# Merging two row blocks' score products into one burst, and the sinks' value product into one stacked split product, in a fused attention, feed-forward and expert kernel

## The chip, the cores and the metric

One core of one Trainium2 chip runs the kernel. The metric is the device time of one execution in microseconds (us); lower is better. Three executions of the kernel before gave 1141.84, 1143.38 and 1145.58 us, median 1143.38 us.

## The reference, cut to what matters

Three stages follow each other: attention with a window of 128 positions and 4 sinks (4 batches, 8 heads, 768 positions, head size 64), a feed-forward layer with `h * cos(h)`, and a top-1 mixture of 8 experts. Only the first stage is touched:

```python
scores = scale * np.matmul(q, k.transpose(0, 1, 3, 2))
keep = is_sink | in_window
scores = np.where(keep, scores, -1000000000.0)
scores = scores - np.max(scores, axis=-1, keepdims=True)
a = np.exp(scores)
a = a / (np.sum(a, axis=-1, keepdims=True) + 1e-09)
return np.matmul(a, v)
```

`is_sink` holds for the first key positions, `in_window` for the last 128 up to the query's own. Everything is float32.

## The kernel before, in words

The tokens are worked on in eight halves, numbered `hb` from 0 to 7: batch `hb // 2`, and in it the first or the second 384 positions (`half = hb % 2`). A half has three row blocks of 128 queries (`t`) and four pairs of heads (`pr`). One attention pair passes through three stages, all of them generators that `attn_front` (L392) makes:

- the front: q and k are loaded, transposed on TensorE, and copied out of PSUM. From the fourth half on (`hb >= STACK`, STACK is 3) they are split in a rounded part and a rest, both in fp32r (`qT[0]`, `qT[1]`, `kT[0]`, `kT[1]`).
- `mid` (L476): `scores` (L490) is called once for each row block. It takes one PSUM bank per head, issues the products for both heads (three per head where q and k are split), and then one VectorE operation per head (L502) that adds the mask, negates, and takes the row's extremum. A row block has 272 keys (128 before, 16 sinks' places, 128 own). In a first half, block 0 has its own 128 keys alone, and block 1 has 272. Six exponentials on ScalarE follow.
- `rest` (L520): VectorE normalizes (L525 on; for `hb < 3` GpSimd multiplies), TensorE transposes the probabilities (`pt`), and the sinks' part goes a way of its own. A copy `pc` (L575) gathers the sinks' columns of both heads (16 each, 32 together), one transpose per row block goes to `pz` (L578), ScalarE copies it to `sp` (L579), and a product with `vs_n` (values of the sinks, one head's in rows 0 to 15 and columns 0 to 63, the other's in rows 16 to 31 and columns 64 to 127) opens the accumulation in `po` (L592). It is a float32 product for each head, into 64 of the 128 partitions. It covers 384 columns in a second half (three row blocks) and 128 columns in a first half (block 2 only, `t0 = 2`; the sinks of blocks 0 and 1 lie in their windows). The products of values and probabilities (L596) are added to the same bank.

`vs_n2` and `sp2` are two buffers each, taken in turn by pairs (`pr % 2`); zeros are written into them once at the start. The sinks' values are loaded into `vs_n` by a DMA on SP's queue (L433).

What sets the order: from the third half on the sequence is written out as mid of a pair, front of the next pair, rest of the pair. Between the `yield`s of this sequence steps of the feed-forward layer of the half before are woven in (`run_ffn`, L1015 on), in proportion to the weight that each yield gives (`steps(hb)`). A step of the feed-forward layer has 12 products `hp` of 384 columns, VectorE and ScalarE operations on `ch` (L142, L145, L688, L148), a rounded part `g_h` on ScalarE, a rest `g_l` on GpSimd, and two steps later 12 products `y` of 512 columns. Then the framework orders each engine's instructions at compile time, by program order and by a model of when each is ready, and places the waits. All of PSUM's eight banks are shared out; from the second half on the attention and the routing take three of them in turn (`ps_a`, L113).

TensorE's operations pass through the helper `mm` (L135, recorded as L136); VectorE's and GpSimd's through `ts`, `stt` and `tt` (L140 to L148).

Of the kernel before, what the change touches and what calls it, by code (L numbers as in the profile page):

```python
# [11 lines left out]
F32 = DT.float32  # L12
F32R = DT.float32r
# [3 lines left out]
AF = mybir.ActivationFunctionType  # L17
ALU = mybir.AluOpType
AX = mybir.AxisListType

P = 128
# [15 lines left out]
STACK = 3  # L37
# [24 lines left out]
def kernel(  # L62
# [17 lines left out]
    B, H, S, D = q.shape  # L80
# [5 lines left out]
    HALF = S // 2  # L86
    NQ = HALF // P
# [4 lines left out]
    NS = 16  # L92
    SEG = P + NS
    W3 = 2 * P + NS
    SCALE = 1.0 / math.sqrt(D)
# [39 lines left out]
    def mm(o, l, r, start, stop):  # L135
        PE.matmul(o, l, r, start=start, stop=stop)  # L136
# [10 lines left out]
    def tt(e, o, a, b, op):  # L147
        e.tensor_tensor(out=o, in0=a, in1=b, op=op)  # L148
# [92 lines left out]
    sp2 = [apool.tile([P, HALF], F32, name=f"sp{i}") for i in range(2)]  # L241
    for i in range(2):
        DVE.memset(vs_n2[i], 0.0)
        POOL.memset(sp2[i], 0.0)
# [68 lines left out]
    def steps(hb):  # L313
        return STEPS_0 if hb <= 1 else STEPS_1
# [80 lines left out]
    def attn_front(hb, pr):  # L395
# [8 lines left out]
        def folded(t):  # L404
            return whole and (half == 1 or t > 1)

        vs_n, sp = vs_n2[pr % 2], sp2[pr % 2]
        n_ps = [0]

        def psb(name):  # L410
            if hb > 0 or not extra:
                return ps_a(name)
            n_ps[0] += 1
            return ps_y(n_ps[0] % NQ, name)
# [59 lines left out]
        def mid():  # L474
            nonlocal mx, sm, Pb, Pt, cols
            kf = [t.rearrange("p t s -> p (t s)") for t in kT]  # L476
            if extra:
                Pb = [[pb_x[2 * t + j][:, 0:W3] for j in range(2)] for t in range(NQ)]
            else:
                Pt = late_pool().tile([P, NQ, 2, W3], F32, name="Pb2") if hb >= PB2 and pr % 2 else apool.tile([P, NQ, 2, W3], F32, name="Pb", bufs=PBB)  # L480
                Pb = [[Pt[:, t, j] for j in range(2)] for t in range(NQ)]
            mx = apool.tile([P, 2 * NQ], F32, name="mx", bufs=2)
            sm = apool.tile([P, 2 * NQ], F32, name="sm", bufs=2)

            def cols(t):
                if half == 0:
                    return (SEG, W3, 0) if t == 0 else (0, W3, (t - 1) * SEG)
                return 0, W3, t * SEG

            def scores(t, js):  # L490

                c0, c1, o = cols(t)
                w = c1 - c0
                qs = slice(t * P, (t + 1) * P)
                ps = {j: psb("ps") for j in js}
                parts = ((0, 0), (0, 1), (1, 0)) if stack else ((0, 0),)
                for n, (x, y) in enumerate(parts):
                    for j in js:
                        mm(ps[j][:, 0:w], qT[x][hr[j], qs], kf[y][hr[j], o:o + w], n == 0, n == len(parts) - 1)
                for j in js:  # L500
                    i = 2 * t + j
                    DVE.tensor_tensor_reduce(  # L502
                        out=Pb[t][j][:, c0:c1], in0=ps[j][:, 0:w], in1=masks[:, min(half * NQ + t, 2), c0:c1],
                        scale=-SCALE, scalar=3.0e38, op0=ALU.add, op1=ALU.min, accum_out=mx[:, i:i + 1])

            for t in range(NQ):
                if hb >= PAIRED:
                    scores(t, (0, 1))
                    yield 2 * steps(hb)[1]
                else:  # L510
                    for j in range(2):
                        scores(t, (j,))
                        yield steps(hb)[1]
            for t in range(NQ):
                for j in range(2):
                    c0, c1, _ = cols(t)
                    i = 2 * t + j
                    ACT.activation(out=Pb[t][j][:, c0:c1], in_=Pb[t][j][:, c0:c1], func=AF.Exp, scale=-1.0,  # L518
                                   bias=mx[:, i:i + 1], accum_out=sm[:, i:i + 1])
            yield steps(hb)[2]  # L520
        def rest():
# [44 lines left out]
                    POOL.tensor_copy(rb[t].rearrange("p (j d) -> p j d", d=D),  # L566
                                     sm[:, 2 * t:2 * t + 2].unsqueeze(2).to_broadcast([P, 2, D]))
            t0 = 2 if half == 0 else 0
            pc = apool.tile([P, NQ, 2, NS], F32, name="pc")
            if extra:  # L570
                for t in range(t0, NQ):
                    for j in range(2):
                        POOL.tensor_copy(pc[:, t, j], Pb[t][j][:, P:SEG])
            else:
                (POOL if hb < NPOOL else DVE).tensor_copy(pc[:, t0:], Pt[:, t0:, :, P:SEG])  # L575
            pz = psb("pz")
            for t in range(t0, NQ):
# [816 lines left out]
```

## Time and profile before

| what | value |
|---|---|
| median of three executions | 1143.38 us (1141.84 to 1145.58) |
| profiled execution, its own time | 1143.94 us |
| its span, first to last instruction | 1142.2 us |
| granted TensorE clock, mean | 0.996 |
| TensorE (PE) busy | 1103.6 us, 97% |
| VectorE (DVE) busy | 678.3 us, 59% |
| ScalarE (ACT) busy | 602.5 us, 53% |
| GpSimd (POOL) busy | 224.5 us, 20% |
| DMA | mean 99 GB/s |

A busy share is taken over the whole span. The four stretches of the kernel are the first halves' attention with the weight conversion (0 to about 231 us), the halves 3 to 7 with the feed-forward layer woven in (about 231 to 690 us), the feed-forward layer alone with the first expert's weights (690 to 1000 us) and the experts (from 1000 us). In rows of the timeline, the time given for a matmul is its own duration through a pipeline, and the next one starts before it ends: what an instruction costs TensorE is read from the distance of starts. A row with "x4" is four instructions of one kind one behind the other; a float32 product is two instructions.

### The profile page before, as it was taken

Reading aid. Unit: us, or ns where it says so; the run is one execution under the profiler, and the core shown is the slowest. Engines: PE = TensorE matmul, PEld = TensorE weight load, DVE = VectorE, ACT = ScalarE, POOL = GpSimd, SP = SyncE. Lnnn points to the kernel's source line nnn. Section 1 sums busy time; section 2 is a strip of 40 time slices with the busy share of each in tenths; the row PEclk is TensorE's granted clock in tenths of the full one; section 3 lists DMA queues with packets and bytes.
Section 4 is the critical chain, followed back from the end, with each engine's and each line's share of the span. In section 5 each row is a group of like instructions: output and inputs, shape, how many; then the busy total and the mean of one; then the engine's idle time right before and its main releaser. Section 6 shows DMA issues by size and latency. Waiting matters only on the chain.

```text
span 1142.2 us, 20840 instructions
## 1 busy us (share of the span) xinstructions
PE 1103.6 (97%) x6624; PEld 928.0 (81%) x6624; DVE 678.3 (59%) x2126; ACT 602.5 (53%) x1239; POOL 224.5 (20%) x273
## 2 busy tenths in 40 slices
PE   5989999999999999999999999999999999999995
PEld 3667777888888878888888879999889998899984
DVE  6778888666876766776676774746742125522210
ACT  5878887656665566665657553434322225422221
POOL 1232224211111111111111111322121211221110
PEclk9999999999999999999999999999999999999998
DMA  6567665422332322323233223633151115111110
GB/s 150 151 197 196 195 195 158 109 73 68 95 74 76 105 72 64 108 70 75 63 104 79 62 75 102 230 93 89 60 203 40 57 58 184 41 58 39 40 43 23
DMA packets 136083, 113.40 MB, mean 99 GB/s; under 512 B 95727, under 2 KB 103919, under 8 KB 135920
## 3 DMA queue, kind: packets, MB, share of 16 engines
q1 hardware_dynamic: 131600, 97.87, 30.3%
q0 software_dynamic: 4320, 13.65, 3.7%
q8 instruction: 66, 1.08, 0.4%
q14 instruction: 97, 0.79, 0.2%
HBM read 151.06 MB, written 19.67 MB: 149 GB/s over the span
## 4 chain that ended last, share of the span: by engine, by line
PE 85%; DVE 5%; DMA 5%; ACT 2%; issue 1%; POOL 1%; SPq 0%; DVEq 0%; POOLq 0%; ACTq 0%
PE hp L136 23%; PE y L626 22%; PE m_h L136 10%; PE m_y L136 10%; PE ps L136 5%; PE po L136 5%; DMA out_dram<-m_ot,m_ids 3%; DMA cv_in<-in_moe_w_in_dram 1%; PE pl L754 1%; PE pq L444 1%; PE pt L546 1%; PE yT L743 1%; PE pk L454 1%; PE m_a L1093 1%; PE mh L136 1%
## 5 line engine op out<-in xcount | busy, mean ns | idle before, releaser
L148 POOL TENSOR_TENSOR g_l<-ch,g_h 128x384 fp32r<-128x384 f32 x128 | 132.4, 1035 | 558.2 <-ACT g_h L698 435.4
L136 PE MATMUL hp<-xT_h,wi_h 128*128 128x384 f32 x512 | 188.3, 368 | 2.7 <-DVE ch L148 2.7
L136 PE MATMUL hp<-xT_h,wi_l 128*128 128x384 f32 x512 | 174.5, 341 | 0.0
L136 PE MATMUL hp<-xT_l,wi_h 128*128 128x384 f32 x512 | 174.0, 340 | 0.0
L626 PE MATMUL y<-wo,g_h 128*128 128x512 f32 x384 | 158.6, 414 | 0.0
L626 PE MATMUL y<-wo_l,g_h 128*128 128x512 f32 x384 | 155.6, 405 | 0.0
L626 PE MATMUL y<-wo,g_l 128*128 128x512 f32 x384 | 154.1, 401 | 0.2 <-POOL g_l L148 0.2
L688 ACT ACTIVATE ch<-ch,cols 128x384 f32<-128x384 f32 x128 | 78.7, 616 | 116.6 <-DVE ch L145 116.0
L136 PE MATMUL m_y<-wi_h,hT 128*128 128x512 f32 x416 | 132.5, 393 | 0.7 <-ACT m_ot L1135 0.6
L145 DVE SCALAR_TENSOR_TENSOR hT<-m_h,hT 128x256 fp32r<-128x256 f32 x88 | 37.3, 424 | 151.0 <-ACTq L1287 102.4
L136 PEld LDWEIGHTS hp<-xT_h,wi_h 128*128 128x128 f32 x512 | 96.7, 189 | 18.1 <-issue 7.2
L142 DVE TENSOR_SCALAR ch<-hp 128x384 int32<-128x384 f32 x128 | 70.9, 554 | 59.1 <-PE hp L136 46.3
L698 ACT ACTIVATE g_h<-ch 128x384 fp32r<-128x384 f32 x128 | 66.4, 520 | 67.8 <-DVE ch L148 46.0
L136 PEld LDWEIGHTS hp<-xT_l,wi_h 128*128 128x128 f32 x512 | 97.0, 189 | 3.7 <-issue 0.2
L136 PEld LDWEIGHTS hp<-xT_h,wi_l 128*128 128x128 f32 x512 | 96.7, 189 | 1.2 <-issue 0.9
L148 DVE TENSOR_TENSOR ch<-ch,hp 128x384 f32<-128x384 f32 x128 | 70.4, 550 | 39.9 <-ACT ch L688 39.5
L136 PEld LDWEIGHTS m_y<-wi_h,hT 128*128 128x128 f32 x416 | 78.1, 188 | 17.0 <-issue 1.0
L518 ACT ACTIVATE Pb<-Pb,mx 128x272 f32<-128x272 f32 (+1 forms) x168 | 82.9, 494 | 10.9 <-DVE mx L502 10.0
L626 PEld LDWEIGHTS y<-wo,g_l 128*128 128x128 f32 x384 | 72.2, 188 | 14.8 <-POOL g_l L148 0.8
L626 PEld LDWEIGHTS y<-wo,g_h 128*128 128x128 f32 x384 | 72.4, 189 | 13.8 <-issue 3.3
L502 DVE CUSTOM_DVE_ANT_0 Pb<-ps,masks 128x272 f32<-128x272 f32 (+1 forms) x168 | 63.7, 411 | 31.7 <-PE ps L136 31.2
L136 PE MATMUL ps<-kT,qT 64*128 64x272 f32 (+1 forms) x504 | 72.6, 350 | 8.9 <-ACT kT L468 7.0
(276 smaller groups left out, 2236.0 us busy)
## 6 DMA issues: line engine op xcount, KB each, us to landing
rw<-in_moe_w_dram SPq DMA_DIRECT2D x112, 512.0 KB
wo_l<-wl_scr SPq DMA_DIRECT2D x122, 256.0 KB
cv_in<-in_moe_w_in_dram SPq DMA_DIRECT2D x16, 512.0 KB
cv_out<-in_moe_w_out_dram SPq DMA_DIRECT2D x16, 512.0 KB
y_scr<-yt SPq DMA_DIRECT2D x24, 256.5 KB
xT_h<-xg_h SPq DMA_DIRECT2D x32, 192.0 KB
xT_l<-xg_l SPq DMA_DIRECT2D x32, 192.0 KB
qn<-in_q_dram SPq DMA_DIRECT2D x56, 96.0 KB
```

What stands on the lines that cost most here:

```text
L136: PE.matmul(o, l, r, start=start, stop=stop)
L142: e.tensor_scalar(out=o, in0=i, scalar1=s1, scalar2=s2, op0=op0, op1=op1)
L145: e.scalar_tensor_tensor(out=o, in0=i0, scalar=s, in1=i1, op0=op0, op1=op1)
L148: e.tensor_tensor(out=o, in0=a, in1=b, op=op)
L444: PE.transpose(pq[:, t * P:(t + 1) * P], qn[:, t].rearrange("p j d -> p (j d)"), ident)
L454: PE.transpose(pk[:, t * P:(t + 1) * P], kn[:, t].rearrange("p j d -> p (j d)"), ident)
L502: DVE.tensor_tensor_reduce(out=Pb[t][j][:, c0:c1], in0=ps[j][:, 0:w], in1=masks[:, min(half * NQ + t, 2), c0:c1], scale=-SCALE, scalar=3.0 ...
L518: ACT.activation(out=Pb[t][j][:, c0:c1], in_=Pb[t][j][:, c0:c1], func=AF.Exp, scale=-1.0, bias=mx[:, i:i + 1], accum_out=sm[:, i:i + 1])
L546: PE.transpose(pt2[:, j * P:(j + 1) * P], Pb[t][j][:, SEG:W3], ident)
L626: i = PE.matmul(o, l, r, start=start, stop=stop)
L688: ACT.activation(out=ch, in_=ch, func=AF.Sin, scale=TWO_PI, bias=half_pi)
L698: ACT.activation(out=gh, in_=ch, func=AF.Copy)
```

## The change: what it does

From `hb = 3` on (`stacked`, the same bound as `stack`):

1. `scores` takes a list of row blocks. In a first half (`hb` 4 and 6) blocks 0 and 1 are done in one call: 12 products in one burst, block 0's 128 columns and block 1's 272 behind each other in one bank for each head, and then four VectorE operations. Block 2 stays a call of its own. Second halves stay as they were.
2. The sinks' product is one fp32r product for both heads. `pc3` holds the rounded probabilities twice and the rest once (96 columns in place of 32), so that `sp_r` has 96 rows; `vsr2` holds in rows 0 to 31 the rounded values, in 32 to 63 their rest, and in 64 to 95 the rounded values again. VectorE makes `pc3` with a copy and a subtraction, GpSimd makes `vsr` with two copies and a subtraction for every pair. New tiles are zeroed by GpSimd once, when the front of half 3 is first traced; `sp_r` takes the place of `sp` (same tag).

```diff
+        stacked = hb >= STACK
+        if stacked and not vsr2:
+            for i in range(2):
+                vsr2.append(apool.tile([P, 2 * D], F32R, name=f"vs_r{i}"))
+                sp2[i] = apool.tile([P, HALF], F32R, name=f"sp_r{i}", tag=f"sp{i}")
+                POOL.memset(vsr2[i].bitcast(F32), 0.0)
+                POOL.memset(sp2[i].bitcast(F32), 0.0)
...
-            def scores(t, js):
...
+            def scores(tl, js):
+
                 ps = {j: psb("ps") for j in js}
-                parts = ((0, 0), (0, 1), (1, 0)) if stack else ((0, 0),)
-                for n, (x, y) in enumerate(parts):
+                at_ = 0
+                spans = []
+                for t in tl:
+                    c0, c1, o = cols(t)
+                    w = c1 - c0
+                    spans.append((t, c0, c1, at_, w))
+                    qs = slice(t * P, (t + 1) * P)
+                    parts = ((0, 0), (0, 1), (1, 0)) if stack else ((0, 0),)
+                    for n, (x, y) in enumerate(parts):
+                        for j in js:
+                            mm(ps[j][:, at_:at_ + w], qT[x][hr[j], qs], kf[y][hr[j], o:o + w], n == 0, n == len(parts) - 1)
+                    at_ += w
+                for t, c0, c1, at_, w in spans:
                     for j in js:
...
+            groups = ((0, 1), (2,)) if stack and half == 0 else ((0,), (1,), (2,))
+            for tl in groups:
                 if hb >= PAIRED:
-                    scores(t, (0, 1))
-                    yield 2 * steps(hb)[1]
+                    scores(tl, (0, 1))
+                    yield 2 * len(tl) * steps(hb)[1]
...
-            pc = apool.tile([P, NQ, 2, NS], F32, name="pc")
-            if extra:
+            if stacked:
+                pc = apool.tile([P, NQ, 3, 2, NS], F32R, name="pc3")
+                pv = Pt[:, t0:, :, P:SEG]
+                DVE.tensor_copy(pc[:, t0:, 0:2], pv.unsqueeze(2).to_broadcast([P, NQ - t0, 2, 2, NS]))
+                tt(DVE, pc[:, t0:, 2], pv, pc[:, t0:, 0].bitcast(F32), ALU.subtract)
+                vsr = vsr2[pr % 2]
+                i0, i1, i2 = [slice(i * 2 * NS, (i + 1) * 2 * NS) for i in range(3)]
+                POOL.tensor_copy(vsr[i0], vs_n[i0])
+                POOL.tensor_copy(vsr[i2], vs_n[i0])
+                tt(POOL, vsr[i1], vs_n[i0], vsr[i0].bitcast(F32), ALU.subtract)
...
+            nr = (6 if stacked else 2) * NS
             for t in range(t0, NQ):
-                PE.transpose(pz[0:2 * NS, t * P:(t + 1) * P], pc[:, t].rearrange("p j s -> p (j s)"), ident)
-            ACT.activation(out=sp[0:2 * NS, t0 * P:], in_=pz[0:2 * NS, t0 * P:HALF], func=AF.Copy)
+                pi_ = pc[:, t].rearrange("p g j s -> p (g j s)").bitcast(F32) if stacked else pc[:, t].rearrange("p j s -> p (j s)")
+                PE.transpose(pz[0:nr, t * P:(t + 1) * P], pi_, ident)
+            ACT.activation(out=sp[0:nr, t0 * P:], in_=pz[0:nr, t0 * P:HALF], func=AF.Copy)
...
-            for j in range(2):
+            if stacked:
+                mm(po[:, t0 * P:HALF], vsr2[pr % 2], sp[:, t0 * P:HALF], True, False)
+            for j in range(0 if stacked else 2):
                 mm(po[hr[j], t0 * P:HALF], vs_n[:, j * D:(j + 1) * D], sp[:, t0 * P:HALF], True, False)
```

## Rows read from the trace of the kernel before

**Rows 1.** The page: busy time, share of the span and instructions of each engine.

```profile
PE 1103.6 (97%) x6624; PEld 928.0 (81%) x6624; DVE 678.3 (59%) x2126; ACT 602.5 (53%) x1239; POOL 224.5 (20%) x273
```

**Rows 2.** Windows: length, busy of PE, PEld, DVE, ACT, POOL (instructions), clock, DMA, GB/s.

```profile
231.00:326.00 95.00, 94.85 (x583) 78.67 (x582) 66.80 (x230) 60.86 (x118) 16.36 (x16) 1.00 0.30 79
...
690.00:1000.00 310.00, 306.49 (x1824) 275.86 (x1823) 149.67 (x438) 109.89 (x213) 63.92 (x60) 1.00 0.32 104
```

**Rows 3.** Waits of TensorE, 231 to 690 us: total us, times, longest.

```profile
PE pz L578 <- DVE pc L575: 0.6, 2, 0.5
```

**Rows 4.** Tile sp, 200 to 1000 us: ns min/median/max, first and last start, forms.

```profile
L136 PE MATMUL po<-sp,vs_n x80: 272/486/537, 225.8 to 683.4; 128*64 128x384 f32 x48, 128*64 128x128 f32 x32
```

**Rows 5.** TensorE's timeline at a second half's sinks' product: start, us, instruction.

```profile
250.25 0.34 PE L136 MATMUL hp<-xT_l,wi_h 128*128 128x384 f32 x1
250.42 0.34 PE L136 MATMUL hp<-xT_h,wi_l 128*128 128x384 f32 x1
250.69 0.87 PE L136 MATMUL po<-sp,vs_n 128*64 128x384 f32 x4
251.39 1.47 PE L136 MATMUL po<-pT,vn 128*64 128x128 f32 x16
```

**Rows 6.** TensorE's timeline at a first half's sinks' product.

```profile
345.07 0.44 PE L136 MATMUL po<-sp,vs_n 128*64 128x128 f32 x4
345.34 1.25 PE L136 MATMUL po<-pT,vn 128*64 128x256 f32 x12
```

**Rows 7.** TensorE's timeline at the routing's fp32r products of 192 columns.

```profile
307.01 0.48 PE L136 MATMUL pi<-rB,rA 128*128 128x192 f32 x3
307.33 0.36 PE L136 MATMUL hp<-xT_h,wi_h 128*128 128x384 f32 x1
```

**Rows 8.** TensorE's timeline at the score products of blocks 0 and 1, half 4.

```profile
349.43 0.34 PE L136 MATMUL hp<-xT_h,wi_l 128*128 128x384 f32 x1
349.69 0.55 PE L136 MATMUL ps<-kT,qT 64*128 64x128 f32 x6
350.17 0.44 PE L136 MATMUL hp<-xT_h,wi_h 128*128 128x384 f32 x1
350.45 0.34 PE L136 MATMUL hp<-xT_l,wi_h 128*128 128x384 f32 x1
...
351.59 0.65 PE L136 MATMUL ps<-kT,qT 64*128 64x272 f32 x6
352.17 0.50 PE L626 MATMUL y<-wo,g_h 128*128 128x512 f32 x1
```

**Rows 9.** Timeline: sinks' copy in rows 5's pair; copy and transpose in a first half.

```profile
248.45 0.22 DVE L575 COPY pc<-Pb 128x96 f32<-128x96 f32 x1
...
385.55 0.18 DVE L575 COPY pc<-Pb 128x32 f32<-128x32 f32 x1
...
386.68 0.27 PE L578 MATMUL pz<-ident,pc 128*32 128x128 f32 x1
```

**Rows 10.** TensorE's timeline at the sinks' transposes of rows 5's pair.

```profile
249.04 0.49 PE L578 MATMUL pz<-ident,pc 128*32 128x128 f32 x3
249.28 0.48 PE L626 MATMUL y<-wo,g_h 128*128 128x512 f32 x1
249.60 0.40 PE L626 MATMUL y<-wo_l,g_h 128*128 128x512 f32 x1
```

**Rows 11.** Groups by form on VectorE: busy us, mean ns, idle before.

```profile
L148 DVE TENSOR_TENSOR ch<-ch,hp 128x384 f32<-128x384 f32 x128 | 70.4, 550 | 39.9 <-ACT ch L688 39.5
...
L575 DVE COPY pc<-Pb 128x96 f32<-128x96 f32 x12 | 2.5, 212 | 0.0
...
L148 DVE TENSOR_TENSOR hT<-m_t,hT 128x128 fp32r<-128x128 f32 x8 | 2.3, 289 | 2.1 <-ACT hT L1123 2.1
```

**Rows 12.** Groups by form on GpSimd: busy us, mean ns, idle before.

```profile
L148 POOL TENSOR_TENSOR g_l<-ch,g_h 128x384 fp32r<-128x384 f32 x128 | 132.4, 1035 | 558.2 <-ACT g_h L698 435.4 <-PE ps L136 32.6 <-PE yT L743 28.4
```

**Rows 13.** GpSimd's timeline around the product of rows 5.

```profile
251.09 1.00 POOL L148 TENSOR_TENSOR g_l<-ch,g_h 128x384 fp32r<-128x384 f32 x1 [2.49 <-ACT g_h L698]
```

More of the change, by code (lines that the diff above doesn't have):

```diff
@@ L240 @@
     vs_n2 = [apool.tile([P, 2 * D], F32, name=f"vs_n{i}") for i in range(2)]
-    sp2 = [apool.tile([P, HALF], F32, name=f"sp{i}") for i in range(2)]
+    sp2 = [apool.tile([P, HALF], F32, name=f"sp{i}", tag=f"sp{i}") for i in range(2)]
+    vsr2 = []
     for i in range(2):
@@ L488, in cols @@
                 return 0, W3, t * SEG
-            def scores(t, js):
-                c0, c1, o = cols(t)
-                w = c1 - c0
-                qs = slice(t * P, (t + 1) * P)
+            def scores(tl, js):
                 ps = {j: psb("ps") for j in js}
-                parts = ((0, 0), (0, 1), (1, 0)) if stack else ((0, 0),)
-                for n, (x, y) in enumerate(parts):
-                    for j in js:
[L499 to L504, printed above, removed]
@@ L506, in mid @@
-            for t in range(NQ):
+                at_ = 0
[10 more added lines that the diff above has]
+                    at_ += w
@@ new lines, in scores @@
+                for t, c0, c1, at_, w in spans:
+                    for j in js:
+                        i = 2 * t + j
+                        DVE.tensor_tensor_reduce(
+                            out=Pb[t][j][:, c0:c1], in0=ps[j][:, at_:at_ + w], in1=masks[:, min(half * NQ + t, 2), c0:c1],
+                            scale=-SCALE, scalar=3.0e38, op0=ALU.add, op1=ALU.min, accum_out=mx[:, i:i + 1])
+            groups = ((0, 1), (2,)) if stack and half == 0 else ((0,), (1,), (2,))
+            for tl in groups:
@@ L507, in mid @@
                 if hb >= PAIRED:
-                    scores(t, (0, 1))
-                    yield 2 * steps(hb)[1]
+                    scores(tl, (0, 1))
+                    yield 2 * len(tl) * steps(hb)[1]
                 else:
                     for j in range(2):
-                        scores(t, (j,))
-                        yield steps(hb)[1]
+                        scores(tl, (j,))
+                        yield len(tl) * steps(hb)[1]
             for t in range(NQ):
@@ L568, in rest @@
             t0 = 2 if half == 0 else 0
-            pc = apool.tile([P, NQ, 2, NS], F32, name="pc")
-            if extra:
+            if stacked:
[8 more added lines that the diff above has]
+                tt(POOL, vsr[i1], vs_n[i0], vsr[i0].bitcast(F32), ALU.subtract)
+            else:
+                pc = apool.tile([P, NQ, 2, NS], F32, name="pc")
+            if stacked:
+                pass
+            elif extra:
                 for t in range(t0, NQ):
@@ L590, in rest @@
             po = psb("po")
-            for j in range(2):
+            if stacked:
+                mm(po[:, t0 * P:HALF], vsr2[pr % 2], sp[:, t0 * P:HALF], True, False)
+            for j in range(0 if stacked else 2):
                 mm(po[hr[j], t0 * P:HALF], vs_n[:, j * D:(j + 1) * D], sp[:, t0 * P:HALF], True, False)
```

## The prediction

> **What bounds the kernel now.** I read the page first: TensorE is busy for 97% of the span, no other engine for more than 59% [rows 1]. Since that is an average, I read the stage that the change touches next, the halves 3 to 7. In its first 95 us TensorE is busy for 94.85, VectorE for 66.80 and GpSimd for 16.36, at full granted clock [rows 2]. Then I asked what TensorE waits for between 231 and 690 us: the whole answer is two waits, 0.6 us together, both of the sinks' transposes for the copy `pc` [rows 3]. So here the time is the sum of what TensorE issues, and a change is worth what it takes off that sum, less any wait that it makes. What comes behind has no fixed date: TensorE is busy for 306 of the next 310 us [rows 2], and later loads are issued by the flow of the work, so I let a gain reach the end whole.
>
> **How prices are read.** A matmul's own time overlaps the next one's, so I use distances of starts. An fp32r product of 384 columns costs 0.17 us (250.25 to 250.42) [rows 5].
>
> **The sinks' product, second halves.** The four instructions (two heads, two per float32 product) start at 250.69 and the next product at 251.39: 0.70 us [rows 5]. There are 48 such instructions, 12 pairs [rows 4]. In their place comes one fp32r product of 384 columns with a 128 x 128 stationary side, the shape of `hp`: 0.17 us. The step from `hp` to the 64-column form costs something too, 250.42 to 250.69 is 0.27 us, 0.10 over the usual distance [rows 5]. That step doesn't vanish: it moves behind the new product, since the next `po` products keep their form. So 0.53 us a pair are saved, **6.3 us**. Upper bound of the new price: 0.27 us, if it pays that step a second time; then 5.2 us.
>
> The Trainium skill (TensorEngine Tiling (Array Packing), Theoretical Speedup) speaks against this part: where the stationary side has at most 64 columns, array tiles side by side give up to twice the speed, and the change gives that up. By it the new product would cost double, 0.35 us, and the sum below would lose 2.1 us. Rows 5 fit the tiles' side of it (two heads in 0.70 us); but the new product does both heads in one pass through the block structure of the values, so I don't take the doubled price.
>
> **The sinks' product, first halves.** Four instructions of 128 columns take 0.27 us (345.07 to 345.34) [rows 6], 32 of them, 8 pairs [rows 4]. The new one is an fp32r product of 128 columns. The nearest rows are products of 192 columns, three in 0.32 us, 0.11 each [rows 7]; by columns it would be 0.07. I take 0.08: 0.19 saved, **1.5 us** (bounds 1.3 and 1.6).
>
> **The burst.** Around block 0's six products, 349.43 to 349.69 is 0.26 us and 350.17 to 350.45 is 0.28 us where 0.17 is usual: 0.09 to get into the 64-row form and 0.11 to get out of it. The bodies are 0.48 us for block 0 and 0.58 us for block 1 [rows 8]. In all 8 first-half pairs (halves 4 and 6, four each) these two bursts stand apart, as here. One burst saves one entry and one exit, 0.20 us, **1.6 us** over 8 pairs. Lower bound nothing, if the order at compile time parts the burst; I see no reason for more, as each product loads its own stationary side in either order. Block 0's VectorE operations now wait for block 1's products, and four run together; nothing behind them on VectorE made TensorE wait before [rows 3], so I cost this at nothing. Without that cover the `ch` operations, 0.55 us each [rows 11], are late and TensorE waits for `hp`'s banks. Two banks fewer are taken per pair, which can only ease the turn of three.
>
> **The transposes.** Three cost 249.04 to 249.60 less the 0.23 us of one `y`, 0.33 us [rows 10]. They have 96 stationary columns in place of 32; the moving side, the identity's 128 columns, is the same, so I add nothing (bounds: nothing, and 0.04 us on each of 44, 1.8 us, which is a distance of 0.15 in place of 0.11).
>
> **VectorE's longer chain.** `pc` took 0.21 us for 96 elements. Its successor writes 192, and a subtraction of 96 elements follows (64 and 32 in first halves). The nearest subtraction takes 0.29 us for 128 [rows 11], so I estimate 0.25, and 0.08 for the wider copy: 0.33 us more in front of the transposes. In the pair of rows 5 the copy ended at 248.67 and the transposes began at 249.04 [rows 9, 10], so some 0.1 to 0.2 us of this is covered, and 0.2 stands open, in 12 second-half pairs. First halves have more room: the shortest of their eight leads is 386.68 - 385.73 = 0.95 us [rows 9]. Against a wait: the compile-time order moves the transposes behind more `y` or `hp` products if its model sees the longer chain. Bounds: nothing, and 12 x 0.33 = 4.0 us. I take 0.12 a pair, **1.4 us lost**, nearer to nothing because only two such waits are there now [rows 3].
>
> **GpSimd.** Three operations on 32 x 128 per pair: by columns each is a third of `g_l`, which takes 1.04 us for 384 [rows 12], so some 1.1 us together as an estimate, 20 times. GpSimd is idle for five sixths of the stage [rows 2], and the sinks' values were loaded a pair of heads earlier, so they hide, provided that they stand ahead of the right `g_l` (rival 2). The load of `vs_n` for two pairs later, on SP's queue, now waits for GpSimd's readers in place of TensorE's product, which is no later. Four one-time zeroings in front of half 3, at most 1 us each by `g_l`, are hidden by the same idle time; one waits for the third half's last sinks' product, and at worst 1 us shows.
>
> **The sum.** 6.3 + 1.5 + 1.6 - 1.4 = 8.0 us. The profiled execution took 1143.94 us around a span of 1142.2, so it would take 1135.9. The median of the three runs stands 0.56 us below it, so the time to be measured is 1135.4 us. With all bounds at one side the gain is 9.5, at the other 6.5 - 6.8, about nothing. A measurement of this kernel can tell some 0.3%, 3.4 us.
>
> **Rivals.**
>
> 1. *The wait takes the gain.* If the transposes' place isn't moved, 12 pairs lose 0.33 us and the gain is 5.4 us: 1138.0. If one of the `ch` operations (0.55 us) [rows 11] gets in between VectorE's copy and its subtraction, 0.88 us are lost in 12 pairs, 10.6 us against 9.4: 1144.6, no change. For it: VectorE is busy for 70% of the stage, and the copy already ends when the transposes start. Against it: program order puts the two next to each other.
> 2. *Slower: GpSimd's queue.* The new product waits for three GpSimd operations. In the same pair as above, a `g_l` starts at 251.09, 0.40 us behind the product, having waited 2.49 us for ScalarE [rows 13]. If the three stand behind it in the queue, they are done at 252.09 + 1.1 = 253.2, and the product that was due at 250.69 holds TensorE for 2.5 us. That decides as soon as 4 pairs of 20 have it (10 us against 9.4); with 10 pairs the loss is 25 - 8 = 17 us: 1160. Against it: in program order the three stand ahead of that `g_l`, and their data are there long before.
> 3. *The burst is parted*, or pays for its form inside: the gain lacks 1.6 us and the time is 1137.0. The doubled price of the untiled product would give 1137.5.
>
> **How the numbers follow.** Forecast 0.68 (its own range 1132 to 1139), rival 3 0.08, rival 1 with its first size 0.06, with its second 0.11, rival 2 0.07. Faster by over 0.3% are the first three, 0.82; within 0.3% is the second size of rival 1, 0.11; slower is rival 2, 0.07. The range goes from 1131.5 (the largest gain of 9.5, and 2 us of scatter between executions) to 1141, which takes in rival 3, rival 1's first size and a little of the second; what it leaves out is rival 2, most of rival 1's second size and tails.
>
> **What would show it.** In the profile after, one `po<-sp_r` instruction of 384 columns with 0.17 us to the next start and 0.1 more behind it; 12 `ps` instructions in a row with one entry and one exit; TensorE's waits in that stage still below 2 us; the stage from half 3 to 7 shorter by 8 us and the stretches behind it as long as before. The prediction is wrong if TensorE waits for `pc3` by 0.3 us or more in most pairs, if it waits for `vs_r` at all, or if the stage gets shorter and a later stretch longer.

## The result, and the profile after

The changed kernel takes 1136.2 us (median of six executions, 1133.28 to 1137.13) against 1145.81 us for six executions of the kernel before beside it: ratio 0.9915 [0.9901, 0.9929], faster by 9.6 us. A second set gave 1136.52 us and 0.9919 [0.9903, 0.9934]. The profiled execution has a span of 1134.2 us and took 1136.03 us.

**Page and windows.** The page's line on engines, then the windows with the columns of [rows 2]; beside them stand [rows 1, 2].

```profile
PE 1095.3 (97%) x6564; PEld 928.8 (82%) x6564; DVE 678.1 (60%) x2146; ACT 602.1 (53%) x1239; POOL 247.0 (22%) x337
```

```profile
231.00:326.00 95.00, 94.16 (x573) 78.82 (x572) 68.30 (x235) 60.88 (x118) 20.44 (x28) 1.00 0.31 81
690.00:1000.00 310.00, 306.75 (x1852) 277.14 (x1851) 148.46 (x437) 110.06 (x216) 64.38 (x60) 1.00 0.31 102
```

TensorE has 60 instructions fewer (20 pairs, four turned into one) and 8.3 us less to do, and is as full as it was. GpSimd's 64 new instructions cost it 22.5 us.

**TensorE's waits, 225 to 690 us**, answering to [rows 3]:

```profile
PE pz L608 <- DVE pc L148: 1.0, 3, 0.5
PE pz L608 <- ACT pT L573: 0.6, 1, 0.6
PE pt L561 <- DVE kT L148: 0.5, 1, 0.5
PE pt L561 <- DVE pT L148: 0.5, 1, 0.5
```

2.6 us in place of 0.6. That is more than the 2 us that the prediction set as a sign, but little against the work removed.

**The sinks' way in a second half.** TensorE's timeline, the pair of [rows 5, 10]:

```profile
251.15 0.49 PE L608 MATMUL pz<-ident,pc 128*96 128x128 f32 x3
251.40 0.42 PE L136 MATMUL hp<-xT_h,wi_h 128*128 128x384 f32 x1
...
252.01 0.34 PE L136 MATMUL hp<-xT_h,wi_h 128*128 128x384 f32 x1
252.22 0.44 PE L136 MATMUL po<-sp_r,vs_r 128*128 128x384 f32 x1
252.59 1.52 PE L136 MATMUL po<-pT,vn 128*64 128x128 f32 x16
```

The new product has 0.37 us to the next start, where [rows 5] have 0.70. It stands 1.07 us behind its transposes; in the kernel before it was 1.65 (249.04 to 250.69). That is close: in nine of the 12 second-half pairs TensorE's weight load waits for ScalarE's copy, and there the product has 0.37 us; the other three have 0.27. Of the tile view of `sp_r`, the line on what TensorE waited for:

```profile
  ACT sp_r L609: 2.0, 9
```

**VectorE in that pair**, answering to [rows 9], and its groups by form, answering to [rows 11]:

```profile
249.86 0.30 DVE L587 CAST pc<-Pb 128x192 fp32r<-128x192 f32 x1
250.09 0.54 DVE L145 SCALAR_TENSOR_TENSOR ch<-hp,ch 128x384 f32<-128x384 f32 x1
250.54 0.24 DVE L148 TENSOR_TENSOR pc<-Pb,pc 128x96 fp32r<-128x96 f32 x1
```

```profile
L587 DVE CAST pc<-Pb 128x192 fp32r<-128x192 f32 x12 | 3.5, 292 | 0.0
L148 DVE TENSOR_TENSOR pc<-Pb,pc 128x96 fp32r<-128x96 f32 x12 | 2.9, 244 | 0.0
```

A `ch` operation does get in between copy and subtraction, here and in nine more of the 12 second-half pairs. In this pair 12 `hp` and `y` products stand between the last transpose of the probabilities and the sinks' transposes, where the kernel before has nine, so the longer chain costs TensorE little as a wait.

One first-half pair (half 4's first) went otherwise:

```profile
320.05 1.00 POOL L148 TENSOR_TENSOR g_l<-ch,g_h 128x384 fp32r<-128x384 f32 x1 [4.58 <-ACT g_h L730]
320.17 0.93 DVE L148 TENSOR_TENSOR pc<-Pb,pc 128x32 fp32r<-128x32 f32 x1
320.54 0.60 ACT L573 ACTIVATE pT<-pt 128x512 f32<-128x512 f32 x1
321.24 0.29 PE L608 MATMUL pz<-ident,pc 128*96 128x128 f32 x1 [0.57 <-ACT pT L573]
```

Five other VectorE operations stand between its copy and this subtraction. The subtraction takes 0.93 us, where the other seven first-half pairs have 0.18 to 0.20; it starts 0.12 us behind a `g_l` of GpSimd and ends 0.05 us behind it. The changed kernel's repetition and E6 have the same in this pair (0.94 and 0.93 us). TensorE loses 0.8 us ahead of this transpose. The trace names ScalarE's `pT`, but that ends only 0.04 us after the subtraction, so it doesn't tell which of the two held TensorE.

**First half.** The sinks' product answering to [rows 6], then one burst answering to [rows 8]:

```profile
345.23 0.22 PE L136 MATMUL po<-sp_r,vs_r 128*128 128x128 f32 x1
345.38 1.30 PE L136 MATMUL po<-pT,vn 128*64 128x256 f32 x12
```

```profile
305.62 0.39 PE L658 MATMUL y<-wo,g_l 128*128 128x512 f32 x1
305.94 0.98 PE L136 MATMUL ps<-kT,qT 64*128 64x128 f32 x12
306.84 0.44 PE L136 MATMUL hp<-xT_h,wi_h 128*128 128x384 f32 x1
307.12 0.34 PE L136 MATMUL hp<-xT_l,wi_h 128*128 128x384 f32 x1
```

0.15 us in place of 0.27. The merged body takes 0.90 us (305.94 to 306.84); the two apart take 0.48 + 0.58 = 1.06 [rows 8]. It still pays one step in (305.62 to 305.94, 0.32 us where `y` takes 0.23) and one out.

**GpSimd in the pair above**, answering to [rows 13], and who waited by the tile view of `vs_r`:

```profile
252.73 0.28 POOL L591 CAST vs_r<-vs_n 32x128 fp32r<-32x128 f32 x1 [2.71 <-PE po L136]
253.07 0.29 POOL L592 CAST vs_r<-vs_n 32x128 fp32r<-32x128 f32 x1
253.44 1.00 POOL L148 TENSOR_TENSOR g_l<-ch,g_h 128x384 fp32r<-128x384 f32 x1
254.52 0.45 POOL L148 TENSOR_TENSOR vs_r<-vs_n,vs_r 32x128 fp32r<-32x128 f32 x1
```

```profile
  POOL vs_r L591: 43.8, 16
  PEld pq L452: 4.5, 1
  ACT g_h L730: 0.7, 1
```

The three operations (1.02 us) run right behind the product that frees their buffer (252.22), two pairs ahead of the one that needs them. GpSimd waits for TensorE. TensorE stands in the list once, with the first weight load of the kernel, at 4.5 us; its matmul waits as long for the load of q, in the kernel before too. No later one waits for `vs_r`.

**The same work, before and after.** Spans of different runs can't be laid side by side: the start differs by some us between profiles of one kernel (last section), and the interleaved feed-forward work shifts over any boundary. So I took two landmarks with equal work between them: the start of ScalarE's copy `xT_h<-po` of the third half's last pair, and the start of the last `hp` product of the whole kernel. Call this the woven window; in all fourteen profiles it holds 1287 or 1288 recorded `hp` and 963 `y` products. It goes from 201.11 to 804.3 us before, 603.19 us, and from 202.85 to 798.1 us after, 595.25 us. Two further profiles of the unchanged kernels gave 603.13 and 595.19. So it repeats to 0.1 us, and the change takes 7.9 us off it.

All distances of TensorE's starts in it, summed by what starts (us):

| what | before | after | burst alone | sinks alone |
|---|---|---|---|---|
| `hp` and `y` | 484.58 | 482.06 | 483.15 | 483.85 |
| scores `ps` | 33.96 | 32.70 | 32.68 | 33.90 |
| sinks' product | 10.52 | 5.38 | 10.51 | 5.36 |
| values' products `po` | 26.24 | 27.25 | 26.26 | 27.24 |
| transposes `pt` | 10.57 | 10.25 | 10.23 | 10.67 |
| transposes `pz` | 3.16 | 3.30 | 3.17 | 3.36 |
| all others | 34.16 | 34.31 | 34.18 | 34.43 |
| sum | 603.19 | 595.25 | 600.18 | 598.81 |

### The profile page after: what moved, and what is told of

Read it like the earlier page. It is cut to its first block, busy times and chain, and to the rows that moved or that the text cites. A ratio compares the mean times of both kernels' runs of the same rounds, so it can differ in the third digit from the quotient of the medians.

```text
span 1134.2 us, 20810 instructions
## 1 busy us (share of the span) xinstructions
PE 1095.3 (97%) x6564; PEld 928.8 (82%) x6564; DVE 678.1 (60%) x2146; ACT 602.1 (53%) x1239; POOL 247.0 (22%) x337
## 4 chain that ended last, share of the span: by engine, by line
PE 85%; DVE 5%; DMA 4%; ACT 2%; issue 1%; POOL 1%; SPq 0%; DVEq 0%; POOLq 0%; ACTq 0%
PE hp L136 23%; PE y L658 23%; PE m_h L136 10%; PE m_y L136 9%; PE ps L136 5%; PE po L136 5%; DMA out_dram<-m_ot,m_ids 3%; PE pl L786 1%; PE pq L452 1%; PE mh L136 1%; PE yT L775 1%; PE pt L571 1%; DMA cv_in<-in_moe_w_in_dram 1%; PE pk L462 1%; PE pt L561 1%
## 5 line engine op out<-in xcount | busy, mean ns | idle before, releaser
L136 PE MATMUL m_y<-wi_l,hT 128*128 128x512 f32 x208 | 81.0, 390 | 0.0
```

## The experiments

Every edit is against the changed kernel. The columns are the ratio to the kernel before with its 95% interval, the median (beside the kernel before's on the same chip), and the woven window (less the 603.19 us before).

| run | ratio | median, before's (us) | window (us) |
|---|---|---|---|
| E1 burst alone | 0.9958 [0.9945, 0.9972] | 1142.58, 1146.62 | 600.18 (-3.0) |
| E2 sinks alone | 0.9942 [0.9928, 0.9955] | 1139.78, 1146.62 | 598.81 (-4.4) |
| E3 sinks last | 0.9908 [0.9895, 0.9922] | 1136.45, 1146.62 | 594.78 (-8.4) |
| E4 one float32 product | 0.9947 [0.9934, 0.9961] | 1141.11, 1146.62 | 599.82 (-3.4) |
| kernel before again | 1.0002 [0.9987, 1.0017] | 1147.82, 1146.87 | 603.13 (-0.1) |
| E5 chain twice | 0.9929 [0.9911, 0.9948] | 1140.06, 1146.87 | 599.22 (-4.0) |
| E6 GpSimd twice | 0.9908 [0.9889, 0.9926] | 1137.51, 1146.87 | 596.45 (-6.7) |
| E7 burst in half 2 | 0.9953 [0.9935, 0.9972] | 1141.87, 1146.87 | 594.84 (-8.4) |
| changed kernel again | 0.9919 [0.9903, 0.9934] | 1136.52, 1145.91 | 595.19 (-8.0) |
| E8 one operation | 0.9932 [0.9915, 0.9948] | 1138.2, 1145.91 | 595.25 (-7.9) |
| E9 chain earlier | 0.9888 [0.9871, 0.9904] | 1133.55, 1145.91 | 593.33 (-9.9) |
| E10 earlier and closing | 0.9898 [0.9884, 0.9912] | 1134.24, 1145.91 | 593.42 (-9.8) |

Where the expectations speak of a stage, they mean halves 3 to 7 up to the copy of the last pair, which is shorter than the window by the last half's feed-forward products.

**E1. The burst alone.**

```diff
-        stacked = hb >= STACK
+        stacked = False
```

> The burst alone; the sinks' product stays two float32 products per pair. The prediction's term, one entry and one exit of the 64-row form saved in 8 pairs: 1.6 us faster than before (ratio 0.9986). A second theory, read from the trace after: the body of the twelve products is shorter too (0.90 us from start to next start, where 0.48 and 0.58 stood apart), so 0.35 us a pair, 2.8 us (0.9975). A rival: the burst gives nothing, since TensorE's form change is only moved (ratio 1.000). The distance from the first product of a burst to the next instruction behind it tells the three apart.

The window is 3.0 us shorter, 0.38 us for each of the eight pairs, about twice the 0.20 predicted. The distances say where. Steps into the score products, told by what a `y` or `hp` takes above its usual distance, sum to 4.80 us in 50 places where they were 5.50 in 58; steps out of them 5.13 in 48, from 5.95 in 56. That is 1.5 us, the predicted term. The other part is in the bodies: `ps` itself falls by 1.28 us, 0.16 a pair, the 0.90 against 1.06 above. What is left, 0.2 us, is the transposes `pt` less small losses.

Read start by start from the traces, the 0.16 us stand at the seam of the two bursts. The products of the two heads start 0.003 us apart, so that a burst is a row of twos. Behind the last product of block 0's burst TensorE took 0.20 us to the next start; inside the merged burst it takes 0.11. Behind the first two of block 1's burst it took 0.23; in the merged one 0.17. So a step in costs 0.09 us in front of a burst and 0.05 inside it, a step out 0.11 us behind it and 0.09 inside.

**E2. The sinks alone.**

```diff
-            groups = ((0, 1), (2,)) if stack and half == 0 else ((0,), (1,), (2,))
+            groups = ((0,), (1,), (2,))
```

> The stacked fp32r sinks' product alone; scores are issued per row block as before. By the prediction's terms 6.3 + 1.5 - 1.4 = 6.4 us faster than before (ratio 0.9944). If the two parts add up, this is the measured change (0.9915) less the burst's part: 0.993 to 0.994. A rival: the parts need each other (the burst frees banks or VectorE in time), then this gives under 4 us (0.9965 or more).

4.4 us, less than predicted for this part (6.4). E1 and E2 add up to 7.4 of the 7.9 us, so the two parts are nearly independent. The sinks' distances fall by 5.16 us and the step ahead of them from 1.87 to 0.40, 6.6 us together. Against that the values' products cost 1.0 us more, and the sinks' transposes and the distance ahead of them 0.6; 0.6 lie in smaller kinds. Nor are the 6.6 the whole: the nine waits for `sp_r` are in this kernel too.

**E3. The sinks' product last.** The two value products that cover all columns open the accumulation, the sinks' product closes it.

```diff
-            if stacked:
-                mm(po[:, t0 * P:HALF], vsr2[pr % 2], sp[:, t0 * P:HALF], True, False)
...
+            if stacked:
+                mm(po[:, t0 * P:HALF], vsr2[pr % 2], sp[:, t0 * P:HALF], False, True)
```

> The whole change, but the stacked product closes the accumulation in place of opening it, so that ScalarE's copy in front of it has the products of values and probabilities (1.5 us) as cover; these are put in an order in which the first two cover all columns. Theory: the wait for that copy (2.0 us of weight loads' idle time in 9 pairs, some 0.1 us of TensorE each) goes, and the kernel is 1 to 2 us faster than the changed one (ratio to before 0.990 or less). Rival: the wait is hidden in the step between forms, which stands there anyway, and nothing changes (0.9915); or the last copy of the probabilities is late in its place and it gets slower (above 0.993).

The timeline of the same pair:

```profile
252.85 0.49 PE L608 MATMUL pz<-ident,pc 128*96 128x128 f32 x3
253.28 1.52 PE L136 MATMUL po<-pT,vn 128*64 128x256 f32 x16
254.73 0.44 PE L136 MATMUL po<-sp_r,vs_r 128*128 128x384 f32 x1
255.01 0.34 PE L136 MATMUL hp<-xT_h,wi_h 128*128 128x384 f32 x1
```

All twelve sinks' products of second halves now have 0.27 to 0.29 us, so the wait for `sp_r` is gone. The sinks' sum falls by 0.7 and `hp` and `y` by 1.6 us, but the transposes `pz`, now right in front of the tiled value products, cost 1.5 more (4.84). The window gains 0.5 us; by the ratios it can't be told from the changed kernel.

**E4. One float32 product for both heads**, without split and stacking (the burst stays).

```diff
-        stacked = hb >= STACK
+        stacked = False
...
+            if stack:
+                mm(po[:, t0 * P:HALF], vs_n, sp[:, t0 * P:HALF], True, False)
-            for j in range(0 if stacked else 2):
+            for j in range(0 if stack else 2):
```

> The burst as in the change, but the sinks' product is one float32 product over all 128 output partitions with the block-structured values as they were, without any split: no extra work on VectorE or GpSimd. By the sum of what TensorE issues: two instructions of 384 columns in about 0.65 to 0.70 us, as much as the four tiled ones, so the time is that of the burst alone (0.9975 to 0.9986), and all of the sinks' gain comes from fp32r. Rival by the Trainium skill's rule on tiles (TensorEngine Tiling (Array Packing), Theoretical Speedup): giving up the tiles side by side doubles the product, 0.70 us more in 12 pairs and 0.27 in 8, 10.6 us lost: ratio 1.007.

```profile
253.07 0.34 PE L136 MATMUL hp<-xT_h,wi_l 128*128 128x384 f32 x1
253.25 0.81 PE L136 MATMUL po<-sp,vs_n 128*128 128x384 f32 x2
253.99 1.52 PE L136 MATMUL po<-pT,vn 128*64 128x128 f32 x16
```

0.74 us to the next start where the two tiled heads took 0.70 [rows 5]: 11.65 us over the 20 pairs against 10.51. The step ahead is gone (253.07 to 253.25 is 0.18), and the value products take the 1.0 us more. All in all the window is 0.4 us from E1's: giving up the tiles neither gains nor loses. So the gain of the sinks' part comes from fp32r, which needs the split. This run also tests the rule that spoke against the change, the Trainium skill (TensorEngine Tiling (Array Packing), Theoretical Speedup), up to twice the speed from tiles. Giving the tiles up costs 6% in this pair and 11% over the twenty, not the double, as one pass through the block structure of the values does the work of both heads.

**The kernel before again.**

> The kernel before, unchanged, for a second profile: which stretches scatter between executions. If the stretch up to half 3 (201.1 us in the first profile, 202.9 in the changed kernel's) and the stretch behind half 7 (457.0 and 454.5) scatter by 1 to 2 us with the same kernel, no term may be read from them; if both repeat within 0.3 us, they have to be explained. The stage of halves 3 to 7 should repeat at 484.1 us within 0.5.

Ratio 1.0002, window 603.13: what is read off the window to 0.1 us means something, and a span does not (it was 1147.0 us here and 1142.2 in the first profile).

**E5. VectorE's chain twice.** Copy and subtraction are issued a second time.

```diff
+                DVE.tensor_copy(pc[:, t0:, 0:2], pv.unsqueeze(2).to_broadcast([P, NQ - t0, 2, 2, NS]))
+                tt(DVE, pc[:, t0:, 2], pv, pc[:, t0:, 0].bitcast(F32), ALU.subtract)
```

> The whole change with VectorE's copy and subtraction of the sinks' columns done twice in every pair (same data), so that the chain in front of the transposes grows once more by some 0.5 us. Theory: the order fixed at compile time moves the transposes behind more products of the feed-forward layer, and nothing changes (ratio to before 0.991 to 0.993, the stage at 477 to 478 us). Rival, the prediction's rival 1: TensorE waits by what the chain grows, 12 x 0.3 to 0.5 us, 4 to 6 us lost (0.995 to 0.997, TensorE's waits for pc above 4 us).

The window is 4.0 us longer than the changed kernel's (the intervals of the ratios overlap), and yet TensorE's waits for the chain are 0.9 us (1.0 there). The distances have it: `ps` 35.34 in place of 32.70 us, the rest spread over `hp` and `y` (0.5), `pz` (0.4), the sinks and `yT` (0.3 each). The timeline shows what happened to a score burst:

```profile
494.07 0.97 PE L136 MATMUL ps<-kT,qT 64*128 64x128 f32 x6
495.10 0.44 PE L136 MATMUL po<-sp_r,vs_r 128*128 128x384 f32 x1
495.47 1.52 PE L136 MATMUL po<-pT,vn 128*64 128x128 f32 x16
496.92 0.97 PE L136 MATMUL ps<-kT,qT 64*128 64x128 f32 x6
497.82 0.44 PE L136 MATMUL hp<-xT_h,wi_h 128*128 128x384 f32 x1
```

This burst of twelve was taken apart, with a sinks' product and 16 value products in its middle; each six take 0.9 to 1.0 us, as long as the whole twelve above. The tile view of `ps`, 494.05 to 495.05 us, has three products of block 0 and three of block 1 in the first six:

```profile
L136 PE MATMUL ps<-kT,qT x6: 271/285/333, 494.1 to 494.8; 64*128 64x128 f32 x3, 64*128 64x272 f32 x3
```

That is one head's half of the burst, and no two of its products start 0.003 us apart as the two heads' do. So the burst was parted between the heads, and TensorE paid for each head alone what both cost together. It happened in the first pairs of halves 4 and 6; in both, block 2's six were parted into three and three as well (0.44 us each, where the six take 0.57). That is all of the 2.6 us in `ps`. Here a longer chain was paid in the order that is made at compile time, by a parting of another kind than rival 3's and dearer. Neither the wait nor "covered" describes that, and as a dose of the chain's price the run is confounded.

**E6. GpSimd's three operations twice.**

```diff
+                POOL.tensor_copy(vsr[i0], vs_n[i0])
+                POOL.tensor_copy(vsr[i2], vs_n[i0])
+                tt(POOL, vsr[i1], vs_n[i0], vsr[i0].bitcast(F32), ALU.subtract)
```

> The whole change with GpSimd's three operations on the sinks' values done twice in every pair (same data), 1.0 us more of GpSimd in each. Theory: they run right behind the product of two pairs earlier and are hidden, nothing changes (0.990 to 0.993). Rival, the prediction's rival 2 or the port that VectorE and GpSimd share: g_l or VectorE's operations get late by it and TensorE waits; 20 x 1.0 us is the most, a loss of over 2 us speaks for it (0.994 or more).

TensorE waits for none of them. The ratio is that of the changed kernel. The window is 1.2 us longer, 0.7 of it one wait that is in no other profile (TensorE's waits, 225 to 690 us); the rest isn't assigned:

```profile
PE hp L136 <- DMA xT_h<-xg_h: 0.7, 1, 0.7
```

**E7. The burst in half 2 too**, where the feed-forward steps are already woven in, but GpSimd still normalizes.

```diff
-            groups = ((0, 1), (2,)) if stack and half == 0 else ((0,), (1,), (2,))
+            groups = ((0, 1), (2,)) if hb > 1 and half == 0 else ((0,), (1,), (2,))
```

> The whole change with the burst also in half 2, whose scores are float32 products without a split (two instructions each). If each parted burst costs 0.35 to 0.46 us as in halves 4 and 6, 4 pairs give 1.4 to 1.8 us more (0.990, and the stretch from half 1 to the end of half 2 shorter by as much). Rival: in half 2 TensorE isn't the only bound (it idles for 1.2 of 96 us there) and nothing changes (0.9915).

Slower than the changed kernel: 0.9953 [0.9935, 0.9972]. The window is as short as there, so the loss lies outside it. From the copy of half 2's first pair to that of its last are 69.82 us, where the thirteen profiles with half 2 unchanged have 66.7 to 67.1. That is some 2.9 us of the 4 to 5 by which the median lies above what the changed kernel's ratios give; the profiled execution was the shortest of the seven, and where the rest lies is not shown. TensorE's waits there, 110 to 210 us, in E7 and then in the changed kernel:

```profile
PE pt L571 <- POOL Pb L142: 5.6, 4, 2.1
```

```profile
PE pt L571 <- POOL Pb L142: 1.7, 2, 1.0
```

With both blocks' scores in one burst GpSimd, which multiplies there, becomes the one that TensorE waits for. The same edit pays in halves 4 and 6, where VectorE does that work (their scores are split, too, which these are not).

**The changed kernel again.**

> The changed kernel, unchanged, beside the next three on one chip. Its ratio to before should lie at 0.9915 again (0.990 to 0.993), and the stage of halves 3 to 7, from the end of half 2 to the end of half 7, should repeat at 476.8 us within 0.1.

0.9919, window 595.19.

**E8. One operation in place of two.**

```diff
-                DVE.tensor_copy(pc[:, t0:, 0:2], pv.unsqueeze(2).to_broadcast([P, NQ - t0, 2, 2, NS]))
-                tt(DVE, pc[:, t0:, 2], pv, pc[:, t0:, 0].bitcast(F32), ALU.subtract)
+                DVE.tensor_copy(pc[:, t0:], pv.unsqueeze(2).to_broadcast([P, NQ - t0, 3, 2, NS]))
```

> One VectorE copy of three parts in place of the copy and the subtraction (the rest of the probabilities is left out of the sinks' product, which gets the rounded part in its place), so that the chain in front of the transposes is one operation, as before the change. Theory: in the change the chain costs the second halves what their gain of 0.24 us a pair lacks to the 0.41 forecast, so 12 x 0.15 to 0.3 us come back: the stage at 473 to 475 us. Rival: the order at compile time already hides the chain, and the stage stays within 0.5 us of 476.8.

This kernel leaves the rest of the probabilities out of the sinks' product, so it serves the timing alone. The window is the same to 0.1 us, and the theory was wrong. The order at compile time took up what the chain lost: the single operation takes 0.44 us in second halves, nine products stand ahead of the transposes again where the changed kernel has 12, and TensorE's waits for `pc` are 1.4 us in place of 1.0. The wait for `pT` in half 4's first pair (0.6) is gone. Still there are the nine waits for `sp_r` (2.8 us of its weight loads' idle time) and the distance of 1.07 us between transposes and product in most second-half pairs.

**E9. The chain earlier.** Copy and subtraction stand ahead of the probabilities' transposes in program order, all else the same. This is what E3, E5 and E8 left: the place of the chain.

```diff
+            t0 = 2 if half == 0 else 0
+            if stacked:
+                pc = apool.tile([P, NQ, 3, 2, NS], F32R, name="pc3")
+                pv = Pt[:, t0:, :, P:SEG]
+                DVE.tensor_copy(pc[:, t0:, 0:2], pv.unsqueeze(2).to_broadcast([P, NQ - t0, 2, 2, NS]))
+                tt(DVE, pc[:, t0:, 2], pv, pc[:, t0:, 0].bitcast(F32), ALU.subtract)
             pT = apool.tile([P, 2, NQ * 256], F32, name="pT", bufs=2)
...
-            t0 = 2 if half == 0 else 0
             if stacked:
-                pc = apool.tile([P, NQ, 3, 2, NS], F32R, name="pc3")
-                pv = Pt[:, t0:, :, P:SEG]
-                DVE.tensor_copy(pc[:, t0:, 0:2], pv.unsqueeze(2).to_broadcast([P, NQ - t0, 2, 2, NS]))
-                tt(DVE, pc[:, t0:, 2], pv, pc[:, t0:, 0].bitcast(F32), ALU.subtract)
```

> The copy and the subtraction are moved ahead of the transposes of the probabilities and their copies out of PSUM, right behind the normalization, in the program's order. Theory as for the kernel with one operation: the sinks' transposes find their data ready, and the second halves gain 0.15 to 0.3 us a pair, 2 to 3.5 us in all (ratio 0.3% below the changed kernel's). Rival: VectorE's two operations then delay its copies pT by 0.5 us in front of the products of values, and TensorE waits there instead: no gain, or up to 12 x 0.2 us lost.

The best of all: 1133.55 us, 0.9888, 3.0 us under the changed kernel on the same chip; the window is 1.9 us shorter than there. (The intervals 0.9871 to 0.9904 and 0.9903 to 0.9934 just touch; that it beats the changed kernel rests on the window as well.) TensorE's timeline, the same pair:

```profile
251.15 0.49 PE L609 MATMUL pz<-ident,pc 128*96 128x128 f32 x3
251.39 0.48 PE L659 MATMUL y<-wo,g_l 128*128 128x512 f32 x1
...
252.85 0.40 PE L659 MATMUL y<-wo,g_l 128*128 128x512 f32 x1
253.08 0.34 PE L136 MATMUL po<-sp_r,vs_r 128*128 128x384 f32 x1
253.35 0.44 PE L136 MATMUL po<-pT,vn 128*64 128x128 f32 x4
```

From transposes to product are now 1.93 us, and 0.27 behind it. TensorE's weight loads wait for `sp_r` three times in place of nine, 0.7 us in place of 2.0. The gain adds up: the sinks' product 0.61 us less (4.77), the time that `hp` and `y` take above their usual distance ahead of the transposes back from 2.33 to 1.27 us, which is its value before the change, and ahead of the sinks' product at least 0.2 less. That is all of the 1.9 us. Of the 1.06 us ahead of the transposes, 0.8 are half 4's first pair: there the subtraction takes 0.18 us again, and TensorE doesn't wait. So the second halves gain some 1.0 us, half of the least that was expected of them.

**E10. E9 with the product closing the accumulation in second halves.**

```diff
-            if stacked:
+            closing = stacked and half == 1
+            if stacked and not closing:
...
+            if closing:
+                mm(po[:, t0 * P:HALF], vsr2[pr % 2], sp[:, t0 * P:HALF], False, True)
```

> The same move, and in second halves the sinks' product closes the accumulation (in first halves it opens it, as in the change). From the kernel with the product last in all pairs: its stage was 0.85 us shorter than the changed kernel's. Theory: both gains add up, the stage at 473 us or less, ratio to before below 0.989. Rival: the wait for ScalarE's copy was the same wait as that for the chain, and this is as fast as the move alone.

Window 593.42 against E9's 593.33, 1134.24 us: the gains don't add, as the wait that closing avoids is mostly gone already (0.7 us).

## Why the prediction was right, and where its terms were off

The time, 1136.2 us, is 0.8 us from the one predicted and inside its range; the mechanism of the forecast is the one that the traces show: TensorE's own sum got smaller and no wait took its place. How near the time came is in part luck. The forecast took its 8.0 us off the median of three executions, 1143.38 us; six executions of the kernel before have 1145.81. So the base was 2.4 us low and the gain, 9.6 us as measured, 1.6 us low, and the two errors cancel to 0.8. In the window the sum came out nearly exact, 8.0 predicted and 7.9 us measured, again because errors of both signs cancel:

| step of the prediction | predicted (us) | measured (us) |
|---|---|---|
| sinks' product, both halves | -7.8 | -7.6 |
| burst, steps in and out | -1.6 | -1.5 |
| burst, its body | 0 | -1.3 |
| VectorE's longer chain, at the second halves' transposes | +1.4 | +0.2 |
| waits of the sinks' product for `sp_r` | none | +0.9 |
| one transpose of a first half | 0 | +0.8 |
| transposes `pz` | 0 | +0.1 |
| values' products | none | +1.0 |
| not assigned | none | -0.5 |
| sum | -8.0 | -7.9 |

- **The sinks' product.** 5.14 us of its distances and 1.5 of the step ahead of it (1.87 to 0.38), and 0.94 more that the waits for `sp_r` took back: where nothing is waited for it has 0.27 us in second halves and 0.15 in first, 12 x 0.27 + 8 x 0.15 = 4.44 of the 5.38 us measured. That the step moves behind the product was right: 0.27 is the 0.17 of an fp32r product and 0.10.
- **The term that was too small is the burst's.** "I see no reason for more" was wrong: the forecast read the steps in and out from the products around a burst, and 0.16 us of them lie inside it, behind its first two products and its last. Merging saves that too. E1 has it, 1.28 us in `ps`. With it the burst is worth 3.0 us, not 1.6.
- **VectorE's chain.** The operations were well priced (292 and 244 ns, against 0.29 and 0.25). The wait that was named, at the second halves' transposes, grew by 0.2 us alone, since the order at compile time moved ten of the 12 behind more products. Two costs without a term came instead: 0.94 us in the waits of the sinks' product for `sp_r`, and 0.8 at half 4's first transpose, where the forecast saw 0.95 us of room. (The 0.2 and the 0.8 are what `hp` and `y` take more ahead of the transposes, 1.27 to 2.33 us.) That 1.4 stands for 2.0 is luck. E8 shows that the waits for `sp_r` don't hang on the chain's length, and E9 gets most of the 2.0 back without shortening it. Why the order puts the sinks' product three or four products behind its transposes, where the kernel before has six, was not tried.
- **The values' products** had no term. They cost 0.05 us more a pair in E2 and E4 alike, wherever the sinks' product isn't tiled. Start by start they stand behind the first two of the value products, 0.15 us where it was 0.10. In the kernel before, the tiled sinks' product had them (0.37 us behind its first two instructions, 0.32 behind the second two). So this is the part of the step in that lies inside a burst: the step moved as forecast, but its price was read without that part.
- **Transposes, GpSimd, the load of `vs_n`:** nothing, as costed. 96 columns to load take 125 ns where 32 took 95, and `pz` sums to 3.30 us in place of 3.16.
- **Rival 1.** Its argument against itself was wrong: a `ch` operation does stand between copy and subtraction, in ten of 12 second-half pairs. What saved the forecast is what it says of VectorE's chain, that the transposes move behind more `y` or `hp`; TensorE waits 1.0 us for the chain, in three pairs.
- **Rival 2** fell by E6 and by the trace. Its place was wrong in kind: the operations stand right behind the product of two pairs earlier, more than a pair ahead of need. What GpSimd may have cost is something else, the 0.93 us subtraction beside a `g_l` above; the `g_l` was there before, and no run moved it alone.
- **Rival 3** didn't come. E5 shows that a burst can be parted, between the heads, at some 1 us each and not at the 0.20 of the forecast.
- **The signs.** TensorE's waits in the stage are 2.6 us, above the 2 that were set. It waits for `pc3` in three pairs, not in most, and not for `vs_r`. The stage of halves 3 to 7 is 7.3 us shorter, not 8, and no later stretch is longer.
- **Whole and end.** The medians fell by 9.6 us, 1.7 more than the window. In the two profiles 1.1 us are a stall in the experts' part that is gone (last section); the rest is within what the start and the end scatter.

## What to carry to other kernels

When one engine is full, sum the distances of its starts by kind between two landmarks with equal work: that repeats to 0.1 us here, and tells parts of 1 us apart that spans can't. Form changes are worth removing twice over, for the step in and out as the neighbours show it (0.20 us) and for the part inside the burst, at its first two products and its last (0.16 us). Where two heads' products start together, an order that parts the heads costs as much again. And when a consumer waits though its chain was shortened in vain, move the chain ahead in program order before making it shorter.

## What the runs showed that I had not expected

- **A stall at the experts' end.** From the start of the last `m_a` product to that of the last `m_y` are 24.3 to 24.8 us in the three profiles whose TensorE has 6624 instructions (before, its repetition, E1) and 23.5 us in the eleven with 6564 or 6584. It is a gap in front of the last page's first `m_h` product. The timeline of the kernel before, then of the changed one:

```profile
1115.91 0.39 PE L136 MATMUL m_y<-wi_h,hT 128*128 128x512 f32 x1
1117.11 0.47 PE L136 MATMUL m_h<-wi_h,m_x 128*128 128x512 f32 x1 [0.81 <-ACT m_ot L1135]
```

```profile
1108.88 0.39 PE L136 MATMUL m_y<-wi_h,hT 128*128 128x512 f32 x1
1109.11 0.39 PE L136 MATMUL m_h<-wi_h,m_x 128*128 128x512 f32 x1
```

  1.20 us from one start to the next against 0.23, in code that no edit touches. The trace names ScalarE's `m_ot` in two of the three and "issue" in the third. That it goes with the number of instructions is all that is shown; the cause wasn't tried.
- **The start scatters, the middle doesn't.** The copy of half 2's last pair starts at 201.11 us in one profile of the kernel before and at 204.77 in another, and half 2's first pair is already 3.65 us apart; from there to the window's end the two agree to 0.1 us.
